# One head's exponentials on VectorE in 76 bursts instead of 52, with scratch in four places and an order planned by a model

## The chip, the cores and the metric

The kernel runs on one core of one Trainium2 chip. The metric is the device time of one execution in microseconds (us). A core has TensorE (PE: matmuls, and PEld for its weight loads), VectorE (DVE), ScalarE (ACT), GpSimd (POOL) and SyncE (SP, which here only issues DMA). Matmul results land in PSUM, eight banks of 128 x 512 float32; everything else is in SBUF.

## The reference, cut to what matters

Sequence 2048, width 1024, 32 heads of 32, bfloat16 inputs.

```
g = sigmoid((x * gate_w).sum(-1))

# a: a diagonal state space model, complex state h of 1024
h_t = Lam_bar * h_{t-1} + B_bar @ x_t
a_t = 2 * Re(C @ h_t) + x_t * Dskip

# b: plain attention, no mask
q, k, v = x @ wqkv
b = softmax(q @ k.T * 32**-0.5) @ v  ->  @ wo

out = g * a + (1 - g) * b
```

Attention needs 32 x 2048 x 2048 exponentials, and they are the largest single job: 1,048,576 for each of 128 partitions, one by one.

## The kernel before: the parts that the argument touches

The kernel is a hand-scheduled list of instructions. Attention is cut into 512 **bursts**: 8 groups of four heads, 8 query blocks of 256, and 8 bursts of 256 keys. A burst makes two tiles of 128 x 1024 scores (z = 0 and z = 1, two heads each). Three PSUM slots of two banks each take turns, bank 6 collects the output, and bank 7 serves all other ("dense") matmuls, one chain of 8 or 16 at a time.

```
# one burst: 8 QK matmuls, then two exps, straight out of PSUM
sl = [(2 * self.p) % 3, (2 * self.p + 1) % 3]
...
def exp(self, B, z, s):
    ...
    if z == 0 and B in DVB:
        self.dve_exp(B, s, p)                      # a "shared" burst
    else:
        self.act(lambda e: e.activation(self.tile[p], ps[:, 2*s:2*s+2, :], ACT.Exp, scale=SCALE), ...)
```

In a **shared burst** (B in DVB) ScalarE takes one head of the first tile, and VectorE computes the other head's exp from integer arithmetic and a polynomial, in five instructions of 128 x 512:

```
def dve_exp(self, B, s, p):
    S.op("act", activation(t[:, 0, :], ps[:, 2*s, :], ACT.Exp, scale=SCALE))             # half an exp
    S.op("dve", tensor_scalar(xi, ps[:, 2*s+1, :], EXP_A, EXP_B, mult, add), "exp_a")    # frees the PSUM slot
    self.dx += [(0.45, tensor_scalar(hi, hi, 0.0, 128.0, max, mult)),                    # exp_b
                (0.69, scalar_tensor_tensor(xw, lo, EXP_C2, lo, add, mult)),             # exp_c
                (0.69, scalar_tensor_tensor(xw, xw, EXP_C1, lo, add, mult)),             # exp_d
                (0.69, scalar_tensor_tensor(t[:, 1, :], xw, EXP_C0, ev, add, mult))]     # exp_f
```
(lambdas and tokens cut; the numbers are the planner's costs in us)

The scratch `xt` (two tiles), `xi` and `xw` of these exps had three homes, which fixed where shared bursts were possible: 52 of the 512.

Besides, VectorE empties bank 7 after each dense chain, normalizes outputs, and runs 32 **scan items** of the state space model, each with 8 products (128x512 bfloat16), two scans and four sums. The dense chains are `proj` and `vproj` (projections), `u` (B @ x), `c` (C @ h, 16 matmuls of 512 columns and 4 of 128 columns for `x * Dskip`, here called **C chains**) and `out`. PE gets a quota of dense matmuls in each burst: 4, but 3 in a shared burst and 5 in the burst before one.

```
period = DPERIOD if p in DVB else PERIOD            # 1.40 or 1.81 us: the planner's whole idea of time
...
quota = 3 if p in DVB else 5 if p + 1 in DVB and not 442 <= p < 459 and (cur is None or cur.left >= 8) else MM_PER_PERIOD
```

Of the kernel before, what the change touches and what calls it, by code (L numbers as in the profile page):

```python
# [928 lines left out]
PERIOD = 1.81  # L929
PE_HEAD = 0.86  # L930
MM_PER_PERIOD = 4
DPERIOD = 1.40
# [6 lines left out]

def dve_bursts():  # L940
    out = []
    for lo, hi, m in ((172, 188, 4), (204, 254, 4), (296, 332, 4), (400, 508, 4)):
        out += [B for B in range(lo, hi) if B % m == 1 and B != 457]
    return out
# [9 lines left out]
class Dense:  # L954

    def __init__(self, pieces, evac, tag):
        self.pieces = pieces
        self.evac = evac
        self.tag = tag
        self.left = sum(w for w, _ in pieces)  # L960
        self.after = 0
        self.extra = 0.0


class FastPath:

    def __init__(self, nc, S, es, d, flag):
# [57 lines left out]
        row6 = self.OT[:, 6, :].rearrange("p (t h n) -> p t h n", t=2, h=2)  # L1025
        row7 = self.OT[:, 7, :]
        hx = [hp[:, r, 4:8, :].rearrange("p a n -> p (a n)") for r in range(2)]
        hx0 = hx[0].rearrange("p (t h n) -> p t h n", t=2, h=2)
        self.xt = [hx0[:, 0], hx0[:, 1], row6[:, 0], row6[:, 1], ub[:, 0], ub[:, 1]]
        self.xi = [hx[1][:, 0:1024].bitcast(I32), row7[:, 0:1024].bitcast(I32), self.ut[:, 0, :].bitcast(I32)]  # L1030
        self.xw = [hx[1][:, 1024:2048].bitcast(F32), row7[:, 1024:2048].bitcast(F32), self.ut[:, 1, :]]
# [39 lines left out]
    def ld_w(self, g, part, eng="sp"):  # L1071
        cb = 1024 * part + 128 * g
        self.dma(lambda e: e.dma_start(self.w[:, g % 2, part], self.wsrc[:, :, cb:cb + 128]), [], [("w", g % 2, part)], "ld_w", eng)
# [251 lines left out]
    def table_ops(self, j):  # L1325
# [5 lines left out]
        over = [("pt", 12 + j // 2), ("pt", 16 + j // 2)]  # L1331
        ops = []
        for k, (x, y) in enumerate(((0, 0), (1, 1), (0, 1), (1, 0))):
            ops.append((0.62, lambda k=k, x=x, y=y: self.dve(lambda e: e.tensor_tensor(prod[:, k], hi[x], lo[y], ALU.mult), self.EFtok, ["gp%d" % k] + (first if k == 0 else []))))
        for r, op in ((0, ALU.subtract), (1, ALU.add)):
            out = Et[:, r, j, :].rearrange("p (a b) -> p a b", a=32)
            ops.append((0.62, lambda r=r, op=op, out=out: self.dve(lambda e: e.tensor_tensor(out, prod[:, 2 * r], prod[:, 2 * r + 1], op), ["gp%d" % (2 * r), "gp%d" % (2 * r + 1)],
                                                                   [("Et", j)] + (over if r == 0 else []) if r == 0 else [("Et", j)])))
# [3 lines left out]
    def item_ops(self, j, ch, n):  # L1342
# [10 lines left out]
        def tt(c, o, a, b, op, r, w):  # L1353
            ops.append((c, lambda: dve(lambda e: e.tensor_tensor(o, a, b, op), r, w)))  # L1354
        tt(0.335, t[0], ure, er, ALU.mult, [u0, Et], [("tq", 0)])
        tt(0.335, t[1], uim, ei, ALU.mult, [u1, Et], [("tq", 1)])
        tt(0.335, t[2], uim, er, ALU.mult, [u1, Et], [("tq", 2)])
        tt(0.335, t[3], ure, ei, ALU.mult, [u0, Et], [("tq", 3)])
        tt(0.6, ut[:, 0, :], t[0], t[1], ALU.add, [("tq", 0), ("tq", 1)], [("ut", 0)])
        tt(0.6, ut[:, 1, :], t[2], t[3], ALU.subtract, [("tq", 2), ("tq", 3)], [("ut", 1)])  # L1360
        rr = self.pf[:, self.RR, j:j + 1].to_broadcast([128, 512])
        for ri in range(2):
            ops.append((1.29, lambda ri=ri: dve(lambda e: e.tensor_tensor_scan(ht[:, ri, :], rr, ut[:, ri, :], self.init[:, ri, j:j + 1], ALU.mult, ALU.add),  # L1363
                                                [("ut", ri), "init", ("pf", self.RR)], [("ht", ri)])))
        if ch < 3:
            ops.append((0.13, lambda: dve(lambda e: e.tensor_copy(self.hl[:, :, j], ht[:, :, 511]), [("ht", 0), ("ht", 1)], [("hl", j)])))
        hre, him = ht[:, 0, :], ht[:, 1, :]
        tt(0.335, t[0], hre, er, ALU.mult, [("ht", 0), Et], [("tq", 0)])
        tt(0.335, t[1], him, ei, ALU.mult, [("ht", 1), Et], [("tq", 1)])
# [729 lines left out]
```

## Time and profile before

| | before |
|---|---|
| median of 4 runs | 940.23 us (939.22 to 940.47) |
| ScalarE busy in the profiled run | 923.2 us of 939.2 |
| VectorE busy | 674.1 us |
| shared bursts | 52 |

From the page of the kernel before: its span, the busy time of each engine (share of the span, number of instructions), and the largest group. A group's line ends with busy time, mean ns of one instruction, and the engine's idle time just ahead of them.

```profile
span 939.2 us, 33706 instructions
...
PE 925.4 (99%) x15316; PEld 520.3 (55%) x15316; DVE 674.1 (72%) x1357; ACT 923.2 (98%) x1034; POOL 10.0 (1%) x39
...
L1651 ACT ACTIVATE f_pt<-f_ps 128x1024 bf16<-128x1024 f32 x892 | 834.0, 1277 | 0.6 <-PE f_ps L1635 0.6
```

PE and ScalarE both read nearly 100%, and neither share can be taken as it stands: matmuls overlap in the record, and so do exps. 892 exps of 1,277 ns would be 1,139 us, while the group was busy for 834. The price of an exp must be read from the spacing, which the chain of waits shows. Columns: start in us, length in us, what the time was spent on.

```profile
806.36 0.49 ACT f_ub L1671
806.85 6.42 ACT f_pt L1651 x7
813.27 0.49 ACT f_ub L1671
```

Seven full exps take 6.42 us (0.917 each), and the half exp of a shared burst 0.49. Four bursts, one of them shared, take 6.91 us, and in this stretch the chain never leaves ScalarE. Elsewhere it does: the pages put 61% of the whole chain on PE and 36% on ScalarE, in the kernel before.

For each exp I also took, from the trace, the time from the end of the exp before to its own end, less 0.917 us (full) or 0.490 (half). What is left over is called a **gap** here: time that ScalarE lost. Over all 1,024 exps the gaps of the kernel before sum to 3.01 us.

### The profile page before, as it was taken

The numbers are of one execution on the slowest core, as the hardware profiler recorded it, in microseconds if no ns is written. First come the engines' busy times: TensorE is split into PE (matmuls) and PEld (weight loads), VectorE is DVE, ScalarE is ACT, GpSimd is POOL, SyncE is SP. The second block draws the span as 40 slices with busy tenths as digits, with TensorE's granted clock in tenths as the row PEclk, the third lists the DMA queues.
The fourth block names the chain that finished last, engine by engine and source line by source line (L and its number), as shares of the span: only waits on it lengthen the run. The fifth ranks groups of instructions, "written<-read, shape, count | busy, mean of one in ns | idle before, by whom it ended". The sixth has DMA issues, their size and how long they took to land.

```text
span 939.2 us, 33706 instructions
## 1 busy us (share of the span) xinstructions
PE 925.4 (99%) x15316; PEld 520.3 (55%) x15316; DVE 674.1 (72%) x1357; ACT 923.2 (98%) x1034; POOL 10.0 (1%) x39
## 2 busy tenths in 40 slices
PE   8999999999999999999999999999999999999996
PEld 4555645565555565555655755544655556555553
DVE  2688888888888766657688766568838466676775
ACT  6999999999999999999999999999999999999996
POOL 2000000000000000000000000000000000000000
PEclk9999999999999999999999999999999999999998
DMA  9659433310133002121023301142201212233412
GB/s 202 104 93 146 76 56 80 74 31 27 34 66 89 30 6 52 41 72 31 19 42 61 75 16 42 42 94 53 53 5 40 73 52 79 80 87 122 115 62 74
DMA packets 157076, 60.90 MB, mean 65 GB/s; under 512 B 145664, under 2 KB 145664, under 8 KB 156928
## 3 DMA queue, kind: packets, MB, share of 16 engines
q1 hardware_dynamic: 154768, 58.16, 28.0%
q8 instruction: 121, 1.98, 0.9%
q10 hardware_dynamic: 2160, 0.53, 0.3%
q14 instruction: 27, 0.22, 0.1%
HBM read 16.79 MB, written 12.58 MB: 31 GB/s over the span
## 4 chain that ended last, share of the span: by engine, by line
PE 61%; ACT 36%; SPq 1%; DMA 1%; issue 0%; DVE 0%; DVEq 0%
ACT f_pt L1651 33%; PE f_ps L1703 17%; PE f_ps L1635 13%; PE f_ps L1446 9%; PE f_ps L1475 9%; PE f_ps L1416 8%; PE f_ps L1434 4%; ACT f_ub L1671 1%; SPq L1068 1%; ACT f_cT_re L1651 1%; DMA f_xT<-in_A_x_dram 1%; ACT f_Et L1651 1%; ACT f_cT_im L1651 1%; PE f_ps L1481 1%; ACT f_OT L1651 0%
## 5 line engine op out<-in xcount | busy, mean ns | idle before, releaser
L1651 ACT ACTIVATE f_pt<-f_ps 128x1024 bf16<-128x1024 f32 x892 | 834.0, 1277 | 0.6 <-PE f_ps L1635 0.6
L1703 PEld LDWEIGHTS f_ps<-f_V,f_pt 128*128 128x128 bf16 x7136 | 228.4, 96 | 115.9 <-issue 94.1
L1703 PE MATMUL f_ps<-f_V,f_pt 128*128 128x33 bf16 x7136 | 279.6, 178 | 0.0
L1635 PE MATMUL f_ps<-f_Q,f_K 32*128 32x256 bf16 x4096 | 230.3, 273 | 3.8 <-ACT f_cT_re L1651 1.2
L1635 PEld LDWEIGHTS f_ps<-f_Q,f_K 32*128 32x128 bf16 x4096 | 80.3, 92 | 158.5 <-issue 73.0
L1446 PE MATMUL f_ps<-f_xT,f_wb 128*128 128x512 bf16 x512 | 131.0, 377 | 0.3
L1416 PE MATMUL f_ps<-f_xT,f_wb 128*128 128x512 bf16 x464 | 119.0, 378 | 0.0
L1363 DVE TENSOR_TENSOR_SCAN f_ht<-f_pf,f_init,f_ut 128x512 bf16<-128x512 f32 x64 | 80.4, 1272 | 0.0
L1475 PE MATMUL f_ps<-f_cT_re,f_hp 128*128 128x512 bf16 x192 | 72.6, 378 | 0.1
L1475 PE MATMUL f_ps<-f_cT_im,f_hp 128*128 128x512 bf16 x192 | 72.6, 378 | 0.0
L1506 PE MATMUL f_ps<-f_wb,f_OT 128*128 128x512 bf16 x252 | 65.7, 379 | 0.1
L1452 DVE CAST f_ub<-f_ps 128x512 bf16<-128x512 f32 x48 | 33.2, 692 | 40.4 <-PE f_ps L1446 40.4
L1434 PE MATMUL f_ps<-f_wb,f_xT 128*128 128x128 bf16 x896 | 59.2, 219 | 0.0
L1446 PEld LDWEIGHTS f_ps<-f_xT,f_wb 128*128 128x128 bf16 x512 | 40.4, 96 | 32.0
L1416 PEld LDWEIGHTS f_ps<-f_xT,f_wb 128*128 128x128 bf16 x464 | 36.3, 96 | 28.0
L1434 PEld LDWEIGHTS f_ps<-f_wb,f_xT 128*128 128x128 bf16 x896 | 50.4, 97 | 0.0
L1672 DVE TENSOR_SCALAR f_ut<-f_ps 128x512 int32<-128x512 f32 x26 | 18.0, 692 | 39.9 <-PE f_ps L1635 39.9
L1354 DVE TENSOR_TENSOR f_tq<-f_ht,f_Et 128x512 bf16<-128x512 bf16 x128 | 45.9, 417 | 0.0
L1354 DVE TENSOR_TENSOR f_ut<-f_tq 128x512 f32<-128x512 bf16 x64 | 42.1, 683 | 0.0
L1488 DVE TENSOR_SCALAR f_Ag<-f_ps,f_gcol 128x512 f32<-128x512 f32 x32 | 24.0, 751 | 18.4 <-PE f_ps L1475 18.4
L1354 DVE TENSOR_TENSOR f_tq<-f_ub,f_Et 128x512 bf16<-128x512 bf16 x96 | 34.6, 417 | 0.0
L1423 DVE CAST f_Q<-f_ps 128x512 bf16<-128x512 f32 x30 | 20.8, 692 | 15.9 <-PE f_ps L1416 15.8
(152 smaller groups left out, 853.6 us busy)
## 6 DMA issues: line engine op xcount, KB each, us to landing
ag_scratch<-f_Ag SPq DMA_DIRECT2D x32, 256.0 KB, 2.5
f_hp<-ag_scratch SPq DMA_DIRECT2D x32, 256.0 KB, 2.9
f_wb<-in_B_wqkv_dram SPq DMA_DIRECT2D x21, 256.0 KB, 4.3
out_dram<-f_xT SPq DMA_DIRECT2D x16, 256.0 KB, 2.1
f_wb<-in_B_wo_dram SPq DMA_DIRECT2D x1, 1024.0 KB, 5.2
f_OT<-f_On SPq DMA_TRANSPOSE x63, 2.3
f_wb<-in_B_wo_dram SPq DMA_DIRECT2D x1, 768.0 KB
f_wb<-in_B_wqkv_dram ACTq DMA_DIRECT2D x2, 256.0 KB, 4.2
```

The costliest lines, as they stand in the source:

```text
L1354: ops.append((c, lambda: dve(lambda e: e.tensor_tensor(o, a, b, op), r, w)))
L1363: ops.append((1.29, lambda ri=ri: dve(lambda e: e.tensor_tensor_scan(ht[:, ri, :], rr, ut[:, ri, :], self.init[:, ri, j:j + 1], ALU.mult, ...
L1416: mms.append((1, lambda e, f, l, a=a: e.matmul(ps[:, bank, :], w[:, g % 2, part, a, :], xT[:, a, 512 * ch:512 * (ch + 1)], start=f, stop=l ...
L1434: m = e.matmul(ps[:, bank, 128 * q:128 * (q + 1)], xT[:, a, 128 * kt:128 * (kt + 1)], w[:, g % 2, 2, a, :], start=(a == 0), stop=(a == 7))
L1446: mms.append((1, lambda e, f, l, a=a: e.matmul(ps[:, 7, :], bT[:, n % 2, ri, a, :], xT[:, a, 512 * ch:512 * (ch + 1)], start=f, stop=l), [ ...
L1452: self.dve(lambda e: e.tensor_copy(self.ub[k][:, ri, :], ps[:, 7, :]), [("bank", 7)], [("ub", k, ri)] + over, "evac_u")
L1475: mms.append((1, lambda e, f, l, j=j, ri=ri: e.matmul(ps[:, 7, :], hp[:, ri, j, cols], cT[ri][:, j, 512 * cb:512 * (cb + 1)], start=f, sto ...
L1488: self.dve(lambda e: e.tensor_scalar(a, ps[:, 7, :], self.gcol[:, 0, tt:tt + 1], None, ALU.mult), [("bank", 7), "g0"], [at], "evac_c")
L1506: mms.append((1, lambda e, f, l, j=j: e.matmul(ps[:, 7, :], OT[:, j, 256 * qb + 128 * r:256 * qb + 128 * (r + 1)], wo[j][0][:, 512 * cb:51 ...
L1635: m = e.matmul(ps[:, 2 * sl[z] + h % 2, 256 * kl:256 * (kl + 1)], K[32 * h:32 * h + 32, g % 2, 128 * kt:128 * (kt + 1)], Q[32 * h:32 * h + ...
L1651: self.act(lambda e: e.activation(self.tile[p], ps[:, 2 * s:2 * s + 2, :], ACT.Exp, scale=SCALE), [("S", s)], [("pt", p)], "exp")
L1703: m = e.matmul(ps[:, 6, o:o + 33], self.tile[p][:, h2, 256 * kl + 128 * qt:256 * kl + 128 * (qt + 1)], V[:, g % 2, 2 * i + kl, h, :], star ...
```

## The change

Its intent: move 24 more half exps from ScalarE to VectorE. For that it needs scratch in more stages of the kernel (the idle half of the weight ring, with loads moved later, and one of two `Ag` buffers), and VectorE time, which has to be planned better. The diff, cut to its core:

```diff
-PERIOD = 1.81
-PE_HEAD = 0.86
+ACT_2 = 0.9165
+ACT_1 = 0.49
+ACT_LAG = 0.466
+QK_LAG = 0.449
+QK_PE = 0.34
+PV_PE = 0.101
+MM_PE = 0.2157
-DPERIOD = 1.40
...
-    for lo, hi, m in ((172, 188, 4), (204, 254, 4), (296, 332, 4), (400, 508, 4)):
-        out += [B for B in range(lo, hi) if B % m == 1 and B != 457]
+DVB_FROM = 69
+DVB_NOT = (69, 73, ... 133, 257, 261, 265, 273, 277, 281, 285, 333, 337, 341, 345, 349, 357, 381, 385, 389, 457)
+    return [B for B in range(DVB_FROM, 508) if B % 4 == 1 and B not in DVB_NOT]
...
     def x_set(self, B):                       # which home the scratch of burst B has
-        return 0 if B < 254 else 1 if B < 392 else 2
+        g, pg = divmod(B, 64)
+        if g == 7 or B >= 433:
+            return 4                          # u ring
+        if pg < 52:
+            return g % 2                      # weight ring
+        return 2 if g < 4 else 3              # state bank, output rows
...
-        tt(0.335, t[0], ure, er, ALU.mult, ...)          # eight products of 128x512 in an item
-        tt(0.335, t[1], uim, ei, ALU.mult, ...)
+        tt(0.602, tq[:, 0:2, :], ub[k], E2, ALU.mult, ...)   # four of 128x1024
...
-        a = self.Ag[:, k % 2, :]
+        a = self.Ag[:, 0, :]
...
-            if pg == 24 and g + 2 < GROUPS:              # when the weights of group g+2 are loaded
+            if pg == (58 if g else 24) and g + 2 < GROUPS:
...
+            T = self.T                                    # the planner's clock, one burst at a time
+            a0 = max(self.act_t, T + QK_LAG) + (ACT_1 if isd else ACT_2)
+            self.act_t = a0 + ACT_2
+            ta = a0 + ACT_LAG
...
+            pe = T + QK_PE + PV_PE * len(head)
...
+            ready = pe + 0.2
+            tp = pe + PV_PE * len(tail) + 0.1
+            self.T = max(ta, tp)                          # ScalarE or PE, whichever is later
+            if ended is not None:
+                nxt_dense = self.T + QK_PE + PV_PE * len(self.quarters.get(p + 1, ()))
+                self.fill(max(ready, nxt_dense - cost - 0.15))   # VectorE's other work, then the evacuation
+            else:
+                self.fill(self.T + (QK_LAG if p + 1 in DVB else 1.0))
```

`fill` gives VectorE its waiting work, instruction by instruction, as long as it ends before the limit by the planner's costs; unfinished exps come first, scan items next, tables last.

More of the change, by code (lines that the diff above doesn't have):

```diff
@@ L937 @@
 EXP_C0 = 3607248267949745.0
+DVB_FROM = 69
+DVB_NOT = (69, 73, 77, 81, 85, 89, 93, 97, 101, 105, 109, 113, 117, 121, 125, 129, 133, 257, 261, 265, 273, 277, 281, 285, 333, 337, 341, 345, 349, 357, 381, 385, 389, 457)
 def dve_bursts():
-    out = []
-    for lo, hi, m in ((172, 188, 4), (204, 254, 4), (296, 332, 4), (400, 508, 4)):
-        out += [B for B in range(lo, hi) if B % m == 1 and B != 457]
-    return out
+    return [B for B in range(DVB_FROM, 508) if B % 4 == 1 and B not in DVB_NOT]
 DVB = set(dve_bursts())
@@ L962, in __init__ @@
         self.extra = 0.0
+        self.group = None
 class FastPath:
@@ L1023, in __init__ @@
         self.tile += [self.cT[ri][:, j, :].rearrange("p (h n) -> p h n", h=2) for j in range(8) for ri in range(2)]
-        row6 = self.OT[:, 6, :].rearrange("p (t h n) -> p t h n", t=2, h=2)
-        row7 = self.OT[:, 7, :]
+        pair = lambda ap: ap.rearrange("p (h n) -> p h n", h=2)
+        half = lambda ap: [pair(ap[:, 0:1024]), pair(ap[:, 1024:2048])]
         hx = [hp[:, r, 4:8, :].rearrange("p a n -> p (a n)") for r in range(2)]
-        hx0 = hx[0].rearrange("p (t h n) -> p t h n", t=2, h=2)
-        self.xt = [hx0[:, 0], hx0[:, 1], row6[:, 0], row6[:, 1], ub[:, 0], ub[:, 1]]
-        self.xi = [hx[1][:, 0:1024].bitcast(I32), row7[:, 0:1024].bitcast(I32), self.ut[:, 0, :].bitcast(I32)]
-        self.xw = [hx[1][:, 1024:2048].bitcast(F32), row7[:, 1024:2048].bitcast(F32), self.ut[:, 1, :]]
+        wx = [self.w[:, x].rearrange("p q a n -> p (q a n)") for x in range(2)]
+        ag = self.Ag[:, 1, :]
+        self.xt = half(wx[0]) + half(wx[1]) + half(hx[0]) + half(self.OT[:, 6, :]) + [ub[:, 0], ub[:, 1]]
+        self.xi = [wx[0][:, 2048:3072], wx[1][:, 2048:3072], hx[1][:, 0:1024], self.OT[:, 7, 0:1024], self.ut[:, 0, :]]
+        self.xi = [ap.bitcast(I32) for ap in self.xi]
+        self.xw = [ag, ag, hx[1][:, 1024:2048].bitcast(F32), self.OT[:, 7, 1024:2048].bitcast(F32), self.ut[:, 1, :]]
         self.tile += self.xt
@@ L1072, in ld_w @@
         cb = 1024 * part + 128 * g
-        self.dma(lambda e: e.dma_start(self.w[:, g % 2, part], self.wsrc[:, :, cb:cb + 128]), [], [("w", g % 2, part)], "ld_w", eng)
+        self.dma(lambda e: e.dma_start(self.w[:, g % 2, part], self.wsrc[:, :, cb:cb + 128]), [], [("w", g % 2, part)] + (self.x_toks(g % 2) if g > 2 else []), "ld_w", eng)
     def ld_b(self, j, n):
@@ L1331, in table_ops @@
         over = [("pt", 12 + j // 2), ("pt", 16 + j // 2)]
+        after = 1 + max(self.tile_end.get(t, 0) for t in (12 + j // 2, 16 + j // 2))
         ops = []
         for k, (x, y) in enumerate(((0, 0), (1, 1), (0, 1), (1, 0))):
-            ops.append((0.62, lambda k=k, x=x, y=y: self.dve(lambda e: e.tensor_tensor(prod[:, k], hi[x], lo[y], ALU.mult), self.EFtok, ["gp%d" % k] + (first if k == 0 else []))))
+            ops.append((0.6, lambda k=k, x=x, y=y: self.dve(lambda e: e.tensor_tensor(prod[:, k], hi[x], lo[y], ALU.mult), self.EFtok, ["gp%d" % k] + (first if k == 0 else []))))
         for r, op in ((0, ALU.subtract), (1, ALU.add)):
             out = Et[:, r, j, :].rearrange("p (a b) -> p a b", a=32)
-            ops.append((0.62, lambda r=r, op=op, out=out: self.dve(lambda e: e.tensor_tensor(out, prod[:, 2 * r], prod[:, 2 * r + 1], op), ["gp%d" % (2 * r), "gp%d" % (2 * r + 1)],
-                                                                   [("Et", j)] + (over if r == 0 else []) if r == 0 else [("Et", j)])))
+            ops.append((0.6, lambda r=r, op=op, out=out: self.dve(lambda e: e.tensor_tensor(out, prod[:, 2 * r], prod[:, 2 * r + 1], op), ["gp%d" % (2 * r), "gp%d" % (2 * r + 1)],
+                                                                   [("Et", j)] + (over if r == 0 else []) if r == 0 else [("Et", j)]), after))
         ops.append((0.0, lambda: self.tabled.append(j)))
@@ L1353, in tt @@
         def tt(c, o, a, b, op, r, w):
-            ops.append((c, lambda: dve(lambda e: e.tensor_tensor(o, a, b, op), r, w)))
-        tt(0.335, t[0], ure, er, ALU.mult, [u0, Et], [("tq", 0)])
-        tt(0.335, t[1], uim, ei, ALU.mult, [u1, Et], [("tq", 1)])
-        tt(0.335, t[2], uim, er, ALU.mult, [u1, Et], [("tq", 2)])
-        tt(0.335, t[3], ure, ei, ALU.mult, [u0, Et], [("tq", 3)])
-        tt(0.6, ut[:, 0, :], t[0], t[1], ALU.add, [("tq", 0), ("tq", 1)], [("ut", 0)])
-        tt(0.6, ut[:, 1, :], t[2], t[3], ALU.subtract, [("tq", 2), ("tq", 3)], [("ut", 1)])
+            ops.append((c, lambda: dve(lambda e: e.tensor_tensor(o, a, b, op), r, w() if callable(w) else w)))
@@ L1361, in item_ops @@
+        E2, E2r = self.Et[:, :, j, :], self.Et[:, ::-1, j, :]
+        tt(0.602, tq[:, 0:2, :], ub[k], E2, ALU.mult, [u0, u1, Et], [("tq", 0)])
+        tt(0.602, tq[:, 2:4, :], ub[k], E2r, ALU.mult, [u0, u1, Et], [("tq", 2)])
+        tt(0.6, ut[:, 0, :], t[0], t[1], ALU.add, [("tq", 0)], [("ut", 0)])
+        tt(0.6, ut[:, 1, :], t[3], t[2], ALU.subtract, [("tq", 2)], [("ut", 1)])
         rr = self.pf[:, self.RR, j:j + 1].to_broadcast([128, 512])
         for ri in range(2):
-            ops.append((1.29, lambda ri=ri: dve(lambda e: e.tensor_tensor_scan(ht[:, ri, :], rr, ut[:, ri, :], self.init[:, ri, j:j + 1], ALU.mult, ALU.add),
+            ops.append((1.192, lambda ri=ri: dve(lambda e: e.tensor_tensor_scan(ht[:, ri, :], rr, ut[:, ri, :], self.init[:, ri, j:j + 1], ALU.mult, ALU.add),
@@ L1364, in item_ops @@
                                                 [("ut", ri), "init", ("pf", self.RR)], [("ht", ri)])))
         if ch < 3:
-            ops.append((0.13, lambda: dve(lambda e: e.tensor_copy(self.hl[:, :, j], ht[:, :, 511]), [("ht", 0), ("ht", 1)], [("hl", j)])))
-        hre, him = ht[:, 0, :], ht[:, 1, :]
-        tt(0.335, t[0], hre, er, ALU.mult, [("ht", 0), Et], [("tq", 0)])
-        tt(0.335, t[1], him, ei, ALU.mult, [("ht", 1), Et], [("tq", 1)])
-        tt(0.335, t[2], hre, ei, ALU.mult, [("ht", 0), Et], [("tq", 2)])
@@ L1371, in item_ops @@
-        tt(0.335, t[3], him, er, ALU.mult, [("ht", 1), Et], [("tq", 3)])
+            ops.append((0.19, lambda: dve(lambda e: e.tensor_copy(self.hl[:, :, j], ht[:, :, 511]), [("ht", 0), ("ht", 1)], [("hl", j)])))
+        tt(0.602, tq[:, 0:2, :], ht[:], E2, ALU.mult, [("ht", 0), ("ht", 1), Et], [("tq", 0)])
+        tt(0.602, tq[:, 2:4, :], ht[:], E2r, ALU.mult, [("ht", 0), ("ht", 1), Et], [("tq", 2)])
         hw = ["warm"] if ch == 0 and j == 0 else []
+        late = lambda: []
         if ch == 2 and j >= 4:
-            hw = self.x_toks(0)
+            late = lambda: self.x_toks(2)
@@ L1375, in item_ops @@
         if b == 1 and j == 0:
             hw = ["fX", "fY", "m_c"] + self.EFtok + ["gp%d" % i for i in range(4)]
-        tt(0.335, hp[:, 0, j, :], t[0], t[1], ALU.subtract, [("tq", 0), ("tq", 1)], [("hp", b, j, 0)] + hw)
-        tt(0.335, hp[:, 1, j, :], t[2], t[3], ALU.add, [("tq", 2), ("tq", 3)], [("hp", b, j, 1)] + hw)
+        tt(0.335, hp[:, 0, j, :], t[0], t[1], ALU.subtract, [("tq", 0)], lambda: [("hp", b, j, 0)] + hw + late())
+        tt(0.335, hp[:, 1, j, :], t[2], t[3], ALU.add, [("tq", 2)], lambda: [("hp", b, j, 1)] + hw + late())
@@ L1482, in d_c @@
                                                                           start=False, stop=False), [("diagD", dt)] + self.xtok(ch)))
-        a = self.Ag[:, k % 2, :]
-        at = ("Ag", k % 2)
+        a = self.Ag[:, 0, :]
+        at = ("Ag", 0)
         tile = 2 * tt + cb
@@ L1589, in plan @@
             self.pt_at[b] = t
+        self.tile_end = {t: e for pr, e in free.items() for t in pr}
         self.ring_at, k, x = {}, 2 * RING, 0
@@ L1610, in x_set @@
     def x_set(self, B):
-        return 0 if B < 254 else 1 if B < 392 else 2
+        g, pg = divmod(B, 64)
[4 more added lines that the diff above has]
+        return 2 if g < 4 else 3
     def x_of(self, B, n):
-        return len(self.tile) - 6 + 2 * self.x_set(B) + n
+        return len(self.tile) - 10 + 2 * self.x_set(B) + n
     def x_toks(self, k):
-        return [(n, len(self.tile) - 6 + 2 * k + t) for n in ("pt", "ptd") for t in range(2)] + [("xi", k), ("xw", k)]
+        t0 = len(self.tile) - 10 + 2 * k
+        assert not any(self.left_in.get(t0 + t, 0) for t in range(2)), (self.p, k)
+        assert not self.dx or self.x_now != k
+        return [(n, t0 + t) for n in ("pt", "ptd") for t in range(2)] + [("xi", k), ("xw", max(k, 1))]
     def pt_of(self, B, z):
@@ L1660, in dve_exp @@
         deps = []
-        if not self.seen_x[k]:
-            self.seen_x[k] = True
-            over = [("hp", k, j, ri) for j in range(8) for ri in range(2)]
+        use = (k, B // 64 if k < 2 else 0)
+        self.x_now = k
+        if use not in self.seen_x:
+            self.seen_x.add(use)
             if k < 2:
-                assert self.c_left[k] == 0
+                assert self.busy_w != B // 64
+                over = [("w", k, q) for q in range(3)] + [("Ag", 1)]
+            elif k < 4:
+                assert self.c_left[k - 2] == 0
+                over = [("hp", k - 2, j, ri) for j in range(8) for ri in range(2)]
             else:
@@ L1672, in dve_exp @@
         self.S.op("dve", lambda e: e.tensor_scalar(xi, ps[:, 2 * s + 1, :], EXP_A, EXP_B, ALU.mult, ALU.add), reads=[("S", s)], writes=[("xi", k)], deps=deps, name="exp_a")
-        I, W = ("xi", k), ("xw", k)
+        kw = max(k, 1)
+        I, W = ("xi", k), ("xw", kw)
         assert not self.dx, (self.p, [c for c, _ in self.dx], self.log[-8:])
@@ L1726, in normalize @@
         if qb == 0 and g >= 6:
-            assert all(self.x_set(B) != 1 or B < U * BURSTS - 8 for B in DVB)
-            x += self.x_toks(1)
+            assert all(self.x_set(B) != 3 or B < U * BURSTS for B in DVB)
+            x += self.x_toks(3)
         self.dma(lambda e: e.dma_start_transpose(self.OT[:, g, 256 * qb:256 * (qb + 1)].rearrange("p (t q) -> p t q", t=2),
@@ L1740, in build @@
         self.holds, self.left_in = {}, {}
-        self.dx, self.seen_x, self.waiting = [], [False] * 3, set()
+        self.dx, self.seen_x, self.waiting, self.x_now, self.busy_w = [], set(), set(), None, None
         self.bg2 = []
@@ L1759, in build @@
                 proj[g][8 + c].after = 16 * c
+            for dn in proj[g]:
+                dn.group = g
         proj[0] = [self.d_qk(0, 0, 2), self.d_qk(0, 0, 3)]
@@ L1787, in build @@
         self.c_end = 0
-        tnext = 0.0
+        self.T = self.act_t = self.evac_t = 0.0
         nq = 0
@@ L1795, in build @@
             second = self.burst(p)
-            t0 = tnext
-            period = DPERIOD if p in DVB else PERIOD
-            tnext = t0 + period
-            if p in DVB:
-                self.dve_t = max(self.dve_t, t0 + 0.35) + 0.70
+            T = self.T
+            isd = p in DVB
+            a0 = max(self.act_t, T + QK_LAG) + (ACT_1 if isd else ACT_2)
+            self.act_t = a0 + ACT_2
+            ta = a0 + ACT_LAG
+            if isd:
+                self.dve_t = max(self.dve_t, T + QK_LAG) + 0.608
+                ta = max(ta, self.dve_t + 0.19)
             nq += len(self.quarters[p])
             ends = nq % 32 == 0 and self.quarters[p]
-            ntail = 0
-            if p % 2 and not ends:
-                ntail = 1 if p in DVB else 2 if p + 2 in DVB else 0
+            ntail = 2 if p % 2 and not ends else 0
+            if isd:
+                ntail = min(ntail, 1)
             head, tail = self.split_pv(p, ntail)
@@ L1808, in build @@
             second()
+            pe = T + QK_PE + PV_PE * len(head)
             if ends:
+                rn = pe + 0.35
+                self.fill(rn)
                 self.normalize(nq // 32 - 1)
-                self.dve_t = max(self.dve_t, t0 + PE_HEAD) + 0.75
+                self.dve_t = max(self.dve_t, rn) + 0.6
             if p >= C_LOADS and p % 4 == 0 and nc < 8:
@@ L1826, in build @@
             wsv = self.d["B_wo"].rearrange("(a p) n -> p a n", p=128)
-            if p == 386:
-                self.dma(lambda e: e.dma_start(self.wo3[0], wsv[:, 0:3, :]), [], ["wo0"] + [("w", 0, q) for q in range(3)], "ld_wo")
+            if p == 437:
+                self.dma(lambda e: e.dma_start(self.wo3[0], wsv[:, 0:3, :]), [], ["wo0"] + [("w", 0, q) for q in range(3)] + self.x_toks(0), "ld_wo")
             if not us and cur is None and not wo1 and p > 400:
@@ L1841, in build @@
             used = 0.0
+            if cur is None:
+                pe = max(pe, self.evac_t)
             quota = 3 if p in DVB else 5 if p + 1 in DVB and not 442 <= p < 459 and (cur is None or cur.left >= 8) else MM_PER_PERIOD
@@ L1879, in build @@
                 used += wt
+                pe += MM_PE if wt else 0.055
                 cur.left -= wt
@@ L1886, in build @@
             self.pv(tail)
-            log.append((p, ended.tag if ended else (cur.tag if cur else None), used, round(self.dve_t - t0, 2), len(self.bg) + len(self.bg2)))
-            early = 0.1 + 0.1 * len(tail) + (0.2 if used < base else 0.0)
-            limit = t0 + (period - early if ended is not None else period + (0.3 if p + 1 in DVB else PE_HEAD))
-            while self.dx:
-                c, fn = self.dx[0]
-                st = max(self.dve_t, t0)
-                if st + c > limit:
-                    break
-                self.dx.pop(0)
-                fn()
-                self.dve_t = st + c
-            while not self.dx and (self.bg or self.bg2):
-                src = self.bg if self.bg and (self.bg[0][2] in self.tabled or not self.bg2) else self.bg2
-                if not src:
-                    break
-                c = src[0][0]
-                st = max(self.dve_t, t0 + 0.3)
-                if c > 0 and st + c > limit:
-                    break
-                src.pop(0)[1]()
-                if c > 0:
-                    self.dve_t = st + c
+            ready = pe + 0.2
+            tp = pe + PV_PE * len(tail) + 0.1
+            self.T = max(ta, tp)
+            log.append((p, ended.tag if ended else (cur.tag if cur else None), used, round(self.T - T, 3), round(self.dve_t - T, 2), len(self.bg) + len(self.bg2), round(self.T, 2), round(tp - T, 3)))
+            if ended is not None:
+                cost = 0.608 if ended.tag in ("proj", "vproj", "u") else 0.668
+                nxt_dense = self.T + QK_PE + PV_PE * len(self.quarters.get(p + 1, ()))
+                self.fill(max(ready, nxt_dense - cost - 0.15))
+            else:
+                self.fill(self.T + (QK_LAG if p + 1 in DVB else 1.0))
+            self.busy_w = cur.group if cur is not None else None
             if getattr(self, "seen_items", 0) != self.items_done:
@@ L1913, in build @@
                 ended.evac()
-                self.dve_t = max(self.dve_t, t0 + period - early + 0.1) + 0.70 + ended.extra
+                st = max(self.dve_t, ready)
+                self.evac_t = st + cost + 0.13
+                self.dve_t = st + cost + ended.extra
         self.log = log
@@ L1917, in build, with fill @@
         self.tail()
+    def fill(self, limit):
+        while True:
+            for src in (self.dx, self.bg, self.bg2):
+                if not src:
+                    continue
+                if src is self.bg:
+                    n = src[0][2]
+                    if n < 8 and n not in self.tabled or n >= 8 and len(self.folded) < 16:
+                        continue
+                if src is self.bg2 and len(src[0]) > 2 and self.p < src[0][2]:
+                    continue
+                c = src[0][0]
+                if c == 0 or self.dve_t + c <= limit:
+                    src.pop(0)[1]()
+                    self.dve_t += c
+                    break
+            else:
+                return
     def tail(self):
@@ L1923, in tail @@
         z = self.ut[:, 1, 0:65]
-        dve(lambda e: e.memset(z, 0.0), [], ["z"] + [("ut", r) for r in range(2)] + self.x_toks(2))
+        dve(lambda e: e.memset(z, 0.0), [], ["z"] + [("ut", r) for r in range(2)] + self.x_toks(4))
         assert not self.dx, (self.p, [c for c, _ in self.dx], self.log[-8:])
```

## The prediction

> **What bounds the kernel now.** ScalarE. The page gives it 923.2 us busy of 939.2 (98%), and the groups view shows 0.6 us of idle time before its 892 main exps. PE reads 99% busy, but its matmuls overlap; its weight loads wait 57.6 us for exps (waits view). The chain of waits gives the price: where one burst in four is shared with VectorE (793 to 925 us) it repeats every 6.90 to 6.91 us, of which seven full exps take 6.42 us (0.917 each) and the half exp 0.49. So sharing a burst saves ScalarE 0.427 us: 512 elements at 0.833 ns, the rate that the Trainium skill states ("ScalarE: Activation LUTs", What ACT_TABLE_LOAD costs); the trace agrees. Over all 1,024 exps I find about 3 us beyond these costs: the kernel runs at its ScalarE floor.
>
> **What the change does.**
> - 24 more half exps leave ScalarE: 24 x 0.427 = 10.2 us off the bounding engine.
> - VectorE gains 24 exps of 0.692 + 0.451 + 0.692 + 0.689 + 0.691 = 3.2 us: +77 us. 256 products of 128x512 (0.335 us apart) become 128 of double width; estimate, same elements, half the fixed cost: 0.6 us each, 8 to 9 us less. VectorE goes from 674 to about 740 us: it has the room (265 us idle, 82 of them just ahead of `exp_a`), though few gaps in 260 to 475 us.
> - PE work is unchanged. A four-burst cycle has 16 dense matmuls (0.216 us each by their spacing in the timeline), four QK groups (about 0.34) and 16 PV quarters (about 0.1): 6.4 us against ScalarE's 6.91. It fits.
> - Weight-ring loads move from 24 to 58 of 64 bursts, some 11 us before the next group; landing takes 4.3 us. One `Ag` buffer replaces two: its store lands in 2.5 us, a C chain takes four bursts.
> - Evacuations and `exp_a` are placed just in time by a model.
>
> **On the critical path.** All 10.2 us, less stalls. Now a shared burst costs about 0.03 us more than its parts, mostly under the C chains (around 600 us, 0.13 us per shared burst) and in 745 to 795 us (cycles of 7.01 to 7.03). More shared bursts now fall under C chains and a fuller VectorE: chained steps of an exp run 0.5 to 0.73 us apart, 0.2 us per burst over the model's costs, which can delay the next `exp_a` and hold a PSUM slot. I allow 1 to 2 us.
>
> 940.35 - 10.2 + 1.4 = about **931.5 us**, range 929.5 to 937. Chances: faster by over 2% 0.01, within 2% 0.97, slower by over 2% 0.02.
>
> **What would show each step.** Right: 76 half exps of 0.49, ScalarE busy about 913 us with idle below 1 us, cycles of about 6.91 us from burst 137 to 253 (263 to 465 us), VectorE busy 735 to 745, less idle per `exp_a` than now (1.6 us), products of 128x1024 spaced about 0.6 us. Wrong: cycles of 7.1 us or more in 263 to 465 us; PE weight loads waiting for VectorE; ScalarE idle before exps; a projection waiting for a load of `f_wb`.
>
> **What would make it wrong.** VectorE late by 0.1 us at each shared burst would cost 76 x 0.1 = 8 us, most of the gain. A DMA queue held up by a load waiting for scratch could cost several us. If the early stalls (about 1.5 us before 130 us) vanish, it lands near 929.5.

## More of the kernel before

At 145 us, where no burst is shared, the chain of the kernel before runs on PE alone (L1703 is the matmul of probabilities and V, PV; L1446 is dense; L1635 is QK):

```profile
144.94 0.50 PE f_ps L1703 x16
145.44 0.87 PE f_ps L1446 x4
146.31 0.46 PE f_ps L1635 x8
146.77 0.50 PE f_ps L1703 x16
```

A burst takes 1.83 us here (144.94 to 146.77), just the price of its two full exps, so ScalarE lost no time.

All runs told of here were in the fast state, with a granted TensorE clock of 0.995 to 0.999.

## The result and the profile after

| | before | after |
|---|---|---|
| median of 4 runs | 940.23 us | 932.44 us (931.59 to 932.63) |
| ratio of the fast runs | | 0.9917 (0.9900 to 0.9935) |
| span of the profiled run | 939.2 us | 930.6 us |
| ScalarE busy | 923.2 us | 914.9 us |
| VectorE busy | 674.1 us | 733.3 us |
| gaps of ScalarE, summed | 3.01 us | 5.44 us |

A ratio here is the mean time of one kernel's fast runs over that of the other's fast runs of the same rounds, so it is not quite the ratio of the medians quoted. The interval lies well clear of 1.

From the page of the kernel after:

```profile
span 930.6 us, 33709 instructions
...
PE 916.7 (99%) x15316; PEld 528.4 (57%) x15316; DVE 733.3 (79%) x1349; ACT 914.9 (98%) x1034; POOL 8.9 (1%) x39
...
L1667 ACT ACTIVATE f_pt<-f_ps 128x1024 bf16<-128x1024 f32 x868 | 817.7, 1227 | 0.6 <-PE f_ps L1651 0.6
```

The chain of waits of the kernel after, where shared bursts lie under projections:

```profile
665.15 0.49 ACT f_wb L1692
665.64 6.42 ACT f_pt L1667 x7
672.06 0.49 ACT f_wb L1692
```

The cycle is 6.91 us, as before; four bursts without a shared one take 7.34. So a shared burst is worth 0.427 us here too, and these bursts (361 to 377) are new.

The sum closes: 24 x 0.427 = 10.24 us off ScalarE, 2.43 us more gaps, and 0.78 us from the stretch before the first exp and after the last one (11.00 and 9.47 us before, 10.80 and 8.90 after; over the runs of the table below these vary by some 0.8 and 1.2 us with nothing changed in them) give 8.59 us, the difference of the two spans.

Where are the new gaps? In three stretches of bursts that hold C chains under shared bursts (1.60 us before, 3.34 after), and in bursts 16 to 63 (0.96 before, 1.74 after). The first 16 bursts have about half a microsecond in both kernels, and everywhere else there are none. In the first kind of place the chain of waits looks quite different. This is one four-burst cycle of the kernel after in bursts 149 to 152, with parts cut (...):

```profile
283.62 0.33 PE f_ps L1651 x8
283.95 0.30 PE f_ps L1725 x8
284.25 0.44 PE f_ps L1481 x2
284.69 0.06 PE f_ps L1487
284.74 0.21 PE f_ps L1481
284.96 0.09 PE f_ps L1725 x4
285.05 0.33 PE f_ps L1651 x8
285.38 0.60 PE f_ps L1725 x20
...
289.10 0.40 PE f_ps L1725 x12
...
290.72 0.21 PE f_ps L1651
```

L1651 is QK, L1725 is PV, L1481 the C products and L1487 the diagonal ones. ScalarE is not in this chain at all. As at 145 us before, that alone shows nothing; what counts is the length. From one QK of a shared burst (283.62) to the next (290.72) it is 7.10 us, more than ScalarE's 6.91, so ScalarE lost 0.19 us in the cycle and something else set it. The rows of the whole cycle sum to 1.3 us of QK, 2.0 of PV, 3.6 of C products and 0.2 of diagonal ones. The busy share hides this: ScalarE reads 28.34 us of 28.40 in this stretch (windows view at the end). The lengths of the exps' records show it: all full exps from 284 to 312 us are recorded with 1.018 to 1.024 us, the shortest there are, and from 658 to 686 us, where ScalarE has no gaps, with 1.214 to 1.375.

The chain can miss a second limit, too. At 757 us, again under C chains, it stays on ScalarE:

```profile
756.47 0.53 ACT f_wb L1692
757.00 6.49 ACT f_pt L1667 x7
763.49 0.53 ACT f_wb L1692
```

Yet the cycle is 7.02 us, 0.11 over ScalarE's price, with records of 1.018 to 1.023 us. That PE is what sets the longer cycles is therefore not read from the chain but tested below, above all by e4.

What VectorE waits for, in the waits view (total us, times, longest); first the kernel before, then the kernel after. L1672 and L1693 are `exp_a`.

```profile
DVE f_ut L1672 <- PE f_ps L1635: 39.9, 26, 5.3
DVE f_hp L1672 <- PE f_ps L1635: 26.1, 17, 2.7
DVE f_OT L1672 <- PE f_ps L1635: 16.5, 9, 2.7
```

```profile
DVE f_wb L1693 <- PE f_ps L1651: 48.7, 38, 2.8
DVE f_ut L1693 <- PE f_ps L1651: 25.6, 18, 1.9
DVE f_OT L1693 <- PE f_ps L1651: 6.6, 4, 2.7
DVE f_hp L1693 <- PE f_ps L1651: 5.7, 6, 1.7
```

VectorE still comes early to its exps: 82.5 us of idle time over 52 exps (1.6 each) before, 86.6 over 76 (1.1 each; 66 of them waited) after. In the same view nothing waits for a load of `f_wb`, neither PE nor VectorE, so no cost of the later weight loads shows.

### The profile page after: what moved, and what is told of

It reads as the page before. It is cut to its first block, busy times and chain, and to the rows that moved or that the text cites. A ratio compares the mean times of both kernels' runs of the same rounds, so it can differ in the third digit from the quotient of the medians.

```text
span 930.6 us, 33709 instructions
## 1 busy us (share of the span) xinstructions
PE 916.7 (99%) x15316; PEld 528.4 (57%) x15316; DVE 733.3 (79%) x1349; ACT 914.9 (98%) x1034; POOL 8.9 (1%) x39
## 4 chain that ended last, share of the span: by engine, by line
PE 61%; ACT 36%; DVE 1%; SPq 1%; DMA 1%; issue 0%; DVEq 0%
ACT f_pt L1667 32%; PE f_ps L1725 17%; PE f_ps L1651 13%; PE f_ps L1452 9%; PE f_ps L1481 9%; PE f_ps L1422 8%; PE f_ps L1440 4%; ACT f_ub L1692 1%; SPq L1076 1%; ACT f_wb L1692 1%; DMA f_xT<-in_A_x_dram 1%; ACT f_Et L1667 1%; ACT f_cT_re L1667 1%; PE f_ps L1487 1%; ACT f_cT_im L1667 0%
## 5 line engine op out<-in xcount | busy, mean ns | idle before, releaser
L1667 ACT ACTIVATE f_pt<-f_ps 128x1024 bf16<-128x1024 f32 x868 | 817.7, 1227 | 0.6 <-PE f_ps L1651 0.6
L1725 PEld LDWEIGHTS f_ps<-f_V,f_pt 128*128 128x128 bf16 x6944 | 240.4, 96 | 136.0 <-issue 97.6
L1725 PE MATMUL f_ps<-f_V,f_pt 128*128 128x33 bf16 x6944 | 293.7, 178 | 0.0
L1651 PE MATMUL f_ps<-f_Q,f_K 32*128 32x256 bf16 x4096 | 225.5, 274 | 3.4 <-ACT f_cT_re L1667 1.2
L1651 PEld LDWEIGHTS f_ps<-f_Q,f_K 32*128 32x128 bf16 x4096 | 75.6, 92 | 120.2 <-ACT f_pt L1667 53.5
L1481 PE MATMUL f_ps<-f_cT_im,f_hp 128*128 128x512 bf16 x192 | 72.6, 378 | 0.0
L1481 PE MATMUL f_ps<-f_cT_re,f_hp 128*128 128x512 bf16 x192 | 72.5, 378 | 0.0
L1693 DVE TENSOR_SCALAR f_wb<-f_ps 128x512 int32<-128x512 f32 x47 | 32.5, 691 | 49.1 <-PE f_ps L1651 48.7
L1458 DVE CAST f_ub<-f_ps 128x512 bf16<-128x512 f32 x48 | 33.0, 687 | 14.6 <-PE f_ps L1452 14.3
L1363 DVE TENSOR_TENSOR f_tq<-f_ht,f_Et 128x1024 bf16<-128x1024 bf16 x64 | 42.0, 684 | 0.2
L1700 DVE SCALAR_TENSOR_TENSOR f_Ag<-f_Ag,f_wb 128x512 f32<-128x512 f32 x47 | 32.5, 691 | 1.4
L1692 ACT ACTIVATE f_wb<-f_ps 128x512 bf16<-128x512 f32 x47 | 33.3, 709 | 0.2
```

The lines of the kernel that those rows point to most:

```text
L1363: ops.append((c, lambda: dve(lambda e: e.tensor_tensor(o, a, b, op), r, w() if callable(w) else w)))
L1458: self.dve(lambda e: e.tensor_copy(self.ub[k][:, ri, :], ps[:, 7, :]), [("bank", 7)], [("ub", k, ri)] + over, "evac_u")
L1481: mms.append((1, lambda e, f, l, j=j, ri=ri: e.matmul(ps[:, 7, :], hp[:, ri, j, cols], cT[ri][:, j, 512 * cb:512 * (cb + 1)], start=f, sto ...
L1651: m = e.matmul(ps[:, 2 * sl[z] + h % 2, 256 * kl:256 * (kl + 1)], K[32 * h:32 * h + 32, g % 2, 128 * kt:128 * (kt + 1)], Q[32 * h:32 * h + ...
L1667: self.act(lambda e: e.activation(self.tile[p], ps[:, 2 * s:2 * s + 2, :], ACT.Exp, scale=SCALE), [("S", s)], [("pt", p)], "exp")
L1692: self.S.op("act", lambda e: e.activation(t[:, 0, :], ps[:, 2 * s, :], ACT.Exp, scale=SCALE), reads=[("S", s)], writes=[("pt", p)], deps=d ...
```

## The experiments

**Theory A**: the gain is the number of half exps taken off ScalarE, times 0.427 us; what is lost again is lost where PE's cycle is longer than ScalarE's, under C chains, and at the start. **Rival B**: the new order and the fused products gave part of the gain. **Rival C**: VectorE, now fuller and planned just in time, is late and makes the gaps.

All results in one table. "Exps" is the time from the end of the first exp to the end of the last one in the profiled run. Gaps are split by place: bursts 16 to 63; the stretches with C chains under shared bursts (128 to 255, 296 to 335, 400 to 441); the other bursts from 64 on. Kernels are compared only within the same rounds. "Before" was 939.99 (e1 to e4), 939.82 (e5 to e8) and 939.90 us (e9 to e11). Every timed kernel but e4 gave a correct result.

| run | shared | median us | ratio to before | exps us | gaps 16-63 | gaps C | gaps other |
|---|---|---|---|---|---|---|---|
| before | 52 | 940.23 | | 918.71 | 0.96 | 1.60 | none |
| after | 76 | 932.44 | 0.9917 | 910.89 | 1.74 | 3.34 | none |
| e1_n52 | 52 | 940.02 | 1.0001 | 918.73 | 1.74 | 1.14 | none |
| e2_drop_c | 70 | 932.99 | 0.9926 | 912.54 | 1.74 | 2.44 | none |
| e3_drop_nc | 70 | 934.39 | 0.9941 | 913.29 | 1.75 | 3.33 | none |
| e4_diag_none | 76 | 928.46 | 0.9877 | 907.34 | 1.74 | none | none |
| e5_pad1 | 76 | 932.05 | 0.9916 | 910.98 | 1.73 | 3.52 | none |
| e6_pad3 | 76 | 983.45 | 1.0466 | 962.32 | 1.73 | 34.47 | 20.19 |
| e7_split | 76 | 940.22 | 1.0003 | 918.72 | 3.08 | 4.22 | 5.74 |
| e8_start | 76 | 932.01 | 0.9917 | 910.26 | 1.02 | 3.31 | none |
| e9_split4 | 76 | 932.97 | 0.9928 | 911.34 | 1.99 | 3.31 | none |
| e10_best | 77 | 931.30 | 0.9909 | 909.54 | 1.04 | 3.31 | none |
| e11_again | 76 | 932.80 | 0.9921 | 911.31 | 1.73 | 3.31 | none |

The first 16 bursts are left out of the gap columns; theirs are 0.2 to 0.9 us in every run, with nothing changed in them.

### e1_n52: everything of the change except the number

```diff
-    return [B for B in range(DVB_FROM, 508) if B % 4 == 1 and B not in DVB_NOT]
+    # the loop of the kernel before: 52 bursts
```

> The new order, the fused products, the four homes, but VectorE takes the 52 bursts of before. Theory A (the gain is the number of half exps taken from ScalarE, times 0.427 us, less PE stalls under the C chains): 24 x 0.427 = 10.2 us longer than the changed kernel, less about 1.7 us of stalls that go with the dropped bursts: about 940.5 to 941 us, and some 3.7 us of ScalarE gaps in the trace instead of 5.4. Rival B (the new order, the fusion or the later evacuations themselves gave a good part of the gain): 937 us or less.

Measured 940.02 us, a little under the 940.5 to 941 expected, and 1.0001 of before. The new order, the fused products, the four homes and the late loads together are worth nothing by themselves, so rival B falls. The homes and the late loads give the other 24 bursts their scratch; whether 76 bursts also need the new order was not run (the fusion they can do without, see e9). The gaps were 3.03 us rather than the 3.7 expected, since 0.5 us fewer lie under the C chains than in the kernel before.

### e2_drop_c and e3_drop_nc: what six shared bursts are worth, here and there

```diff
 DVB_NOT = (...
+           141, 145, 149, 153, 157, 161      # e2: six that lie under C chains
+           353, 361, 365, 369, 373, 377      # e3: six that lie under projections and u chains
```

> The changed kernel without six of its shared bursts that lie under C chains (141 to 161). Theory A (PE is the second limit there, its four-burst cycle is about 7.10 us against ScalarE's 6.91): the six bring only 6 x 0.427 - 0.86 = 1.7 us, so 1.7 us longer than the changed kernel, and the 0.86 us of ScalarE gaps in bursts 128 to 171 gone. Rival (every burst is worth 0.427 us): 2.6 us longer.

> The changed kernel without six of its shared bursts that lie under projections and u chains (353, 361 to 377). Theory A and the rival: 6 x 0.427 = 2.6 us longer, no change of the gaps elsewhere.

In the traces, six bursts under C chains were worth 1.65 us (912.54 - 910.89), six under projections 2.40, or 2.57 without the first 16 bursts, whose gaps happened to be 0.17 us smaller. Without the six under C chains, bursts 128 to 171 had no gaps at all, against 0.86 us. The times agree in direction only (932.99 and 934.39, 1.4 us apart; by the ratios to before, each uncertain by some 1.2 us, six bursts would be worth 0.8 and 2.3 us). By the traces, a shared burst of 141 to 161 thus brings about 0.27 us rather than 0.43.

### e4_diag_none: less work for PE under the C chains (wrong result on purpose)

```diff
-        for q in range(4):
-            dt = 4 * cb + q
-            mms.insert(5 * q + 3, (0, lambda e, f, l, ...: e.matmul(ps[:, 7, 128*q:128*(q+1)], xT[...], self.diagD[:, dt, :], ...)))
```

> Wrong result on purpose: the 128 diagonal products in the C chains (x times Dskip) are left out, so PE has 0.055 us less work for each, about 0.22 us in a four-burst cycle. Theory A (PE sets the 0.04 to 0.13 us gaps at shared bursts under C chains): of the 3.3 us of gaps there in the changed kernel less than 1 us is left, 2.5 us shorter in all (929.5 to 930.5 us). Rival C (VectorE is late with exp_a or with freeing bank 7): the gaps stay, 932 us.

All gaps under C chains went, 3.34 us of them. The time was 928.46 us, 1 us lower than expected, as the expectation left almost 1 us of gaps standing. In the same place as the PE chain above, the chain of waits of this run shows:

```profile
283.52 0.49 ACT f_wb L1688
284.01 6.42 ACT f_pt L1663 x7
290.43 0.49 ACT f_wb L1688
```

The cycle is 6.91 us again, and so are those at 757 us. The planner orders this kernel anew, so a few other instructions moved too, but VectorE's work on the exps was the same. PE's work made those gaps, and rival C falls for them; e5, which loads VectorE instead, adds only 0.2 us to them.

### e5_pad1 and e6_pad3: more VectorE work inside the exps

```diff
+        pad = lambda e: e.tensor_scalar(xw, self.ident[:, 0:1].to_broadcast([128, 512]), 1.0, 0.0, ALU.mult, ALU.add)
-        self.dx += [(0.45, lambda: self.dve(..., "exp_b")),
+        self.dx += [(0.45, lambda: (self.dve(pad, ["ident"], [W], "pad"), self.dve(..., "exp_b"))),     # e5: once, e6: three times
```

> The changed kernel with one more VectorE instruction of 128x512 float32 in each of its 76 exps, ahead of the second step, which the planner does not know of (some 0.4 to 0.6 us each, 30 to 45 us of VectorE in all). Theory A (VectorE is off the critical path, and its idle time ahead of exp_a takes it up): within 1 us of the changed kernel, 932 to 933.5 us. Rival C (VectorE's lateness makes the gaps of ScalarE): 76 times some tenths, 8 us or more longer, 940 us or more.

> The same with three such instructions (90 to 135 us of VectorE more). Theory A: now VectorE's idle time in the shared stretches (about 1 us per cycle at 263 to 327 us, 1.5 us at 327 to 474 us) is used up, so this one must be longer, by 76 x 0.3 to 0.8 us, 955 to 990 us. If VectorE did not matter at all it would stay at 932 to 934 us.

With one pad VectorE was 752.7 us busy (+19, or 0.25 per exp) and the time did not move: 932.05 us. The gaps under C chains were 3.52 instead of 3.34, so the pads cost at most some 0.2 us. The expectation had 30 to 45 us of extra work; the pads were shorter than that. So the kernel after has at least this much room in its shared bursts, and it speaks against harm from the chained steps of an exp that the planner counts too short. With three pads (816.2 us busy, +83) the room is gone: 983.45 us, with new gaps in all stretches with shared bursts and no new ones in bursts 16 to 127, where no burst is shared. In the waits view of that run:

```profile
DVE f_wb L1693 <- PE f_ps L1651: 37.6, 37, 1.8
PEld f_ps L1726 <- DVE f_On L1740: 32.7, 38, 1.1
```

VectorE's spare time ahead of `exp_a` shrank, and PE's PV matmuls (L1726) now wait for VectorE to normalize the output bank (L1740), which stands behind the pads in its queue.

### e7_split and e9_split4: the fused products undone

```diff
# e7: one product of 128x1024 -> two of 128x512, both writing the same token
+                ops.append((c, lambda: [dve(lambda e, i=i: e.tensor_tensor(o[:, i], a[:, i], b[:, i], op), r, w + [("half", i)]) for i in range(2)]))
# e9: each half with its own token, and the sums wait for both, as in the kernel before
+                ops.append((c, lambda: [dve(lambda e, i=i: e.tensor_tensor(o[:, i], a[:, i], b[:, i], op), rd(i), [("tq", n + i)]) for i in range(2)]))
```

> The changed kernel in its own order, but each product of 128x1024 is given as two of 128x512 again: VectorE 8 to 9 us more busy. Theory A: no change of time (within 0.7 us of the changed kernel). Rival C: longer by 1 us or more.

The expectation failed: 940.22 us, 8 us longer, the whole gain of the change. Part of that is my edit: its two halves write one token, so the second waits for a semaphore of the first, and they start 0.450 us apart, not 0.335. A product then costs about 0.18 us more than the fused one (0.450 + 0.335 against the 0.602 at which fused ones follow each other), an estimate of 23 us in all; the page has VectorE at 750.0 us (+17), the rest is waiting. But that is no more than e5 added for nothing. The likely difference is the place. The gaps that this run adds stand mostly where there are no or few shared bursts: 1.2 us in bursts 64 to 127, 1.3 in 256 to 295, 3.2 in 336 to 399. One of the largest (0.66 us, burst 343) in the timeline of that run; in brackets, how long the engine was idle before, and who ended it (rows between these are left out):

```profile
627.17 1.02 PE L1425 MATMUL f_ps<-f_xT,f_wb 128*128 128x512 bf16 x4
628.57 0.68 DVE L1366 TENSOR_TENSOR f_ut<-f_tq 128x512 f32<-128x512 bf16 x1
629.17 0.68 DVE L1432 CAST f_K<-f_ps 128x512 bf16<-128x512 f32 x1
630.21 0.81 PE L1455 MATMUL f_ps<-f_xT,f_wb 128*128 128x512 bf16 x3 [1.00 <-DVE f_K L1432]
631.39 1.02 ACT L1670 ACTIVATE f_pt<-f_ps 128x1024 bf16<-128x1024 f32 x1 [0.56 <-PE f_ps L1654]
```

`f_K` L1432 is the evacuation of bank 7. The chain that it empties (L1425) ends at about 628.2, but the evacuation stands behind a sum of a scan item (L1366) that the planner had fitted in front of it by cost, and starts at 629.17. PE waits 1.00 us for it before the next chain, QK comes late, and then the exp. That gave **theory D**: VectorE has room in the shared bursts, but elsewhere its queue is filled right up to the evacuations.

> Mends the previous split run, whose two halves wrote one token and so waited for each other (0.42 us each, not 0.335): now each half has its own token, as in the kernel before. VectorE gets 128 x 0.07 = 9 us more, all of it in the scan items, and the planner does not know. Theory D (new, after that run: VectorE has room in the shared bursts but is packed without gaps ahead of the evacuations in the stretches without shared bursts, so only what is added there costs time): gaps of ScalarE appear in bursts 16 to 127, 256 to 295 and 336 to 399, and the kernel is 1 to 3 us longer than the changed one. Theory A as first put (VectorE has room everywhere): within 0.5 us.

With proper tokens the halves start 0.335 us apart, VectorE is 740.0 us busy (+7), and the only change of the gaps is 0.25 us in bursts 16 to 63 (1.99 against 1.73 in e11). The time, 932.97 against 932.80 us, is no different. So theory D's expectation of 1 to 3 us failed as well: some 9 us of VectorE work in the items is still absorbed, some 23 us with waits in it are not. The fusion is a convenience to the planner and not what carries the result. That the place matters rests on e5 against e7; e7 adds waits as well as work, so the two are not a clean pair and the place is argued rather than shown; how much of its 8 us is due to the place and how much to the waits stays open.

### e8_start: the gaps at the start

In the kernel after, the largest single gap (0.44 us) is at burst 19. Its chain of waits:

```profile
43.18 0.15 DVE f_pf L1247 x2
43.33 0.13 DVE f_pf L1248
43.46 0.59 DVE f_ub L1458
44.05 0.16 DVE f_pf L1247 x2
44.21 1.01 PE f_ps L1452 x4
45.22 0.33 PE f_ps L1651 x8
```

The evacuation `f_ub` L1458 stands behind small instructions of the parameter math; PE starts its dense matmuls only after it. The planner believed VectorE free when the main loop starts; in truth it has a backlog from the opening.

```diff
         self.T = self.act_t = self.evac_t = 0.0
+        self.dve_t = 1.2
```

> The changed kernel with the planner told that VectorE is 1.2 us behind when the main loop starts (it is told 0 now), so fewer small instructions of the parameter math go ahead of the first evacuation of bank 7. If that evacuation is what holds PE and then ScalarE for 0.44 us at burst 19 of the changed kernel, that gap goes, and the 1.74 us of gaps in bursts 16 to 63 fall by 0.4 to 0.8 us: about 932 us. Rival (the gap has another cause, such as a DMA): it stays at 0.44 us.

The gap at burst 19 is gone, and bursts 16 to 63 have 1.02 us of gaps, as the kernel before had (0.96). The time is 932.01 us, by its ratio to before (0.9917) the same as the kernel after; a change of 0.7 us is at the edge of what five runs show, so this rests on the trace.

### e10_best and e11_again: the version that the experiments point to

```diff
         self.T = self.act_t = self.evac_t = 0.0
+        self.dve_t = 1.2
-DVB_NOT = (..., 389, 457)
+DVB_NOT = (..., 389)                # 77 shared bursts
```

> The changed kernel with the planner's start of 1.2 us for VectorE and with burst 457 shared too (77 in all). Theory A: 0.43 us for the burst and about 0.7 us of early gaps: 1.1 us shorter than the changed kernel in the same call, 931 to 931.5 us.

> The changed kernel once more, to be compared with the other two on the same chip: 932.2 us, give or take 0.4.

931.30 us against 932.80 for the kernel after, and 0.9909 of before against 0.9921. The two intervals overlap (0.9894 to 0.9924 and 0.9908 to 0.9935), so the times alone do not quite settle it. The traces agree: without the first 16 bursts, where e11 happened to lose 0.66 us more, the exps of e10 took 1.11 us less, 0.43 for one more half exp and 0.68 for the early gaps. This version beats both kernels, narrowly.

Tried in the planner only and not run: each of the other 33 excluded bursts, given to VectorE one at a time, breaks one of the planner's own deadlines (scan items not done when their scratch is needed, or dense chains left over at the end); fewer dense matmuls per cycle under C chains did so too or, with the planner's rule that makes up for them, only moved them.

## Why the prediction was right, point by point

- **The time.** 931.5 us with 929.5 to 937 was predicted, 932.44 measured, and 932.80 again (e11). The predicted gain was 10.2 - 1.4 = 8.8 us, the measured one 7.8. The range would have held any gain from 3 to 11 us, so that the time fell into it proves little; the steps below carry more.
- **ScalarE is the bound, and 24 half exps are 10.2 us.** Right. The chain of waits shows 0.427 us per shared burst before and after, and the number alone makes the gain (e1: 1.0001 of before with everything else changed).
- **1.4 us of new stalls.** Too small: the gaps grew by 2.43 us: 1.74 more under the C chains, 0.78 more in bursts 16 to 63, and about 0.1 less before those. The term that was mis-sized is PE's cycle, "6.4 us against ScalarE's 6.91. It fits". The place was named in the prediction; the size was wrong. PE's cycle under C chains is 7.10 us where it is longest, and about 7.01 in other parts of them. The sum left out the diagonal products (four of 0.055 us) and a fixed cost of PV: the chain shows 0.30, 0.40 and 0.60 us for 2, 3 and 5 quarters after QK, so 0.1 us for each such run on top of 0.1 us per quarter, 2.0 us instead of 1.6. With both, the sum is 7.0 us.
- **Cycles of 6.91 us from burst 137 to 253.** Half right. Of the 29 cycles that begin with bursts 137 to 249, 17 took 6.91 to 6.93 us, seven 6.96 to 7.06, and five (149 to 157, 205 and 209) 7.10 to 7.12. The prediction had named cycles of 7.1 us or more here as a sign that it is wrong, and for its step "It fits" they are.
- **VectorE at about 740 us with room to spare.** 733 us, just under the 735 to 745 given, and fused products at 0.602 us. It has room in the shared bursts: 19 us more inside the exps cost at most 0.2 us (e5). That speaks against the named danger, chained steps 0.2 us over the planner's costs; no run took these steps away.
- **Weight loads at 58 and a single `Ag`.** No wait, as predicted: the waits view has none on `f_wb`'s loads, and VectorE waits at `f_Ag` only for PE.
- **The early stalls might vanish.** They grew, by the planner's wrong belief about VectorE at the start (e8).

## What to carry to other kernels

When work is moved off the bounding engine, price it from the spacing of that engine's instructions, and then ask for each stage which engine is next and by how much: here PE's cycle lay 0.2 us above ScalarE's in one stage, and a moved exp was worth 0.27 us there against 0.43 elsewhere. Find the stages where the bounding engine's spacing exceeds its price: neither its busy share nor the engine that the chain of waits names shows them. Here the chain ran on PE where ScalarE lost nothing (145 us before) and on ScalarE where it lost 0.11 us per cycle (757 us after). Which engine is the second limit is settled by taking work away from it (e4) and by adding work to its rival (e5). Idle time of an engine is room only where it lies; test it by adding work in the very place that is in question.

## What the Trainium skill lacked or had wrong

- "ScalarE: Activation LUTs" (What ACT_TABLE_LOAD costs) has 0.833 ns per element, which the traces confirm: 0.427 us for 512 elements. Its fixed cost of an ACTIVATE with immediate scale and bias (186 ns, of which 93 overlap back to back) differs a little: here an exp that had to wait ran for 1.018 us (1024 elements) or 0.597 us (512), a fixed part of about 165 to 170 ns, and back to back they followed each other every 0.917 and 0.490 us, a fixed part of about 64.
- "Perfetto Trace Analysis" (DVE / Act Engine Instruction) says that the record of a ScalarE instruction starts when it begins to execute, so that waiting in the queue stays outside. In these traces the same exp of 128x1024 is recorded with 1.018 to 1.421 us, short where ScalarE waits for PE (1.018 to 1.024 at 284 to 312 us) and longer where exps follow each other without gaps (1.214 to 1.375 at 658 to 686 us, spacing 0.917); so up to 0.4 us of waiting behind the exp before seems to be inside.
- The same page (Identifying the Most-Contended Engine) judges how near TensorE is to its limit by MFU (the share of its peak that the matmuls make use of) and by the busy share of weight loads. In the stretch where PE was the limit (284 to 312.4 us) that was 15.73 of 28.40 us, 55%; where ScalarE was the limit (658 to 686 us) it was 19.07 of 28.00, 68%. Here the second measure points the wrong way: 7.2 of the 19.07 us are weight loads for the 128-column matmuls of a projection. MFU would hardly tell the two stretches apart either: counted from the shapes and numbers in the lines view, the multiplications per us differ by about 1% (an estimate). The windows view of the kernel after shows the two stretches (each line: the stretch, its length, then busy us of PE with its number of instructions, then PEld, DVE, ACT and POOL alike, granted clock, DMA share, GB/s):

```profile
284.00:312.40 28.40, 28.40 (x469) 15.73 (x468) 25.33 (x45) 28.34 (x33) 0.00 (x0) 1.00 0.13 44
658.00:686.00 28.00, 27.97 (x538) 19.07 (x534) 23.55 (x42) 28.00 (x35) 0.00 (x0) 1.00 0.15 26
```

- "VectorE: DVE Perf Modes" (The DRAIN you can't avoid) says of eight copies in a row that a semaphore after each costs nothing extra. For the products here that does not hold: two bfloat16 products of 128x512 started 0.450 us apart with a semaphore between them (e7) and 0.335 without (e9). The same section does say that an instruction which is not held can start earlier; what it lacks is how much earlier, and so what a semaphore costs then.
